# Moving the next tile's transposes, rounding and low part ahead of the roots and the norm, in every z2 block of a gMLP kernel

## The chip, the cores and the metric

The kernel runs on one core of a Trainium2 chip. The core has five engines, each with an instruction queue of its own that runs in order: TensorE (PE) for matrix products, VectorE (DVE), ScalarE (ACT), GpSimd (POOL) and SyncE (SP). In this kernel SP, and POOL for stores, mainly issue DMA transfers between the main memory and the on-chip memory. Engines wait for one another by semaphores. The metric is the device time of one execution in microseconds (us).

## The reference

The network is a layer norm with modulation, a state-space convolution (SSM), a second modulated layer norm, and a gMLP over 2048 tokens of 576 channels. The change lies in the gMLP:

```python
def _B_ref(x, w_in, w_sp, b_sp, w_out):
    z = _gelu(jnp.einsum("bsd,df->bsf", x, w_in))
    z1 = z[..., :Fh]
    z2 = _layernorm(z[..., Fh:], axis=-1)
    g = jnp.einsum("ts,bsf->btf", w_sp, z2) + b_sp[None, :, None]
    return jnp.einsum("bsf,fd->bsd", z1 * g, w_out)
...
h = _layernorm(x, axis=-1) * (1 + cb) + sb
x = x + gb * _B_ref(h, B_w_in, B_w_sp, B_b_sp, B_w_out)
```

Fh is 2304. All is in float32; the kernel reaches that precision with products of 16-bit pairs, a rounded high part and the low part that is left.

## The kernel before

The program has three stages: the SSM (up to about 440 us of the span), **phase A**, which makes the normalised z2 of all tokens and prepares weights (to about 680 us), and **phase B**, which makes z1, the spatial product and the output.

Phase A goes over 16 blocks of 128 tokens, b = 0 to 15. A block has these steps:

- `x1_load` (SP) fetches the 576 channels of a block's rows, four blocks ahead. The rows of blocks 0 to 3 are not loaded that way; they lie together in one large tile, `x1f`, in the pool `xz`. From block 8 on, the same pool's memory takes blocks of the spatial weights (`block_load`).
- `ln2_stats` and `roots` (DVE) make mean and inverse root of the rows' layer norm, and `ln2_rows` (DVE) applies it, two blocks ahead.
- `turn` (PE) transposes the normalised rows of the next block, in five products, into the accumulator tile `pt`, of which there is one. `turn_hi` (ACT) rounds them to 16 bits into the tile `nt`; `turn_lo` (DVE) subtracts to get the low part, and POOL stores `nt` (`n_d` in the profile) for phase B.
- `z2_mm(b, h)` (PE) makes 512 columns of z2 (256 for h = 4) in 14 products from `nt` and the weights `wz`; `z2_gelu(b, h)` (ACT) moves them through the gelu into the z2 tile, 2304 columns wide. z2 tiles come from the pool `zp`, which has two buffers, taken in turn.
- `z2_stats` (DVE) gathers the statistics of the z2 tile in six pieces; `roots(b-1, b+2)` makes the inverse root for the z2 tile of block b-1 and for the rows of block b+2 in one run of 16 small instructions; for even tiles `z2_diff` (DVE) forms a difference of the two halves; `z2_norm` (ACT) normalises the tile in place.
- `z2_store` (POOL) issues two transfers that bring the tile to main memory (`z_d` in the profile). Only when they have landed is its buffer free.

The loop body of block b therefore works on tile b, finishes tile b-1 and prepares the rows of b+1 and b+2. Between these steps stand side jobs, called by `do(b, k)` at six places: scaling and splitting of other weights (`side_sum`, `side_hi`, `side_lo`, `win_scale`, `scales_sp`), squares of weights for their norms (`norm_sp`, `norm_out` on ACT, at A0, ahead of the block's first gelu; their loads are issued at A1 of the block before), and the spatial weights' split (`wsp_sums`, `wsp_hi`, `wsp_lo`). The place `PE` holds the small products with `ones` that add up squares over partitions, and the few DVE instructions behind them.

In phase A the object `self.nc` is `self.tied`: the planner keeps every instruction of an engine in program order. Their line in the profile is L132, that of the helper, so that they are told apart by tile names: `z` is a z2 tile (written by the gelu from `pz`, by the norm from `z`), `nt` the rounded rows, `vh`, `rq`, `rx`, `r`, `nm` are the roots, `n` the normalised rows, `bsz` the z2 statistics, `wsst` the weights that are squared.

Before the change, block 1 has an order of its own: there `turn`, the second gelu, `turn_hi` and `turn_lo` stand ahead of `roots`. In all later blocks they stand behind `z2_norm`.

Of the kernel before, what the change touches and what calls it, by code (L numbers as in the profile page):

```python
# [9 lines left out]
F32 = mybir.dt.float32  # L10
# [12 lines left out]
FH = 2304  # L23
# [779 lines left out]
class Mlp:  # L803
# [419 lines left out]
    def z2_gelu(self, b, h):  # L1223
        n = min(512, FH - 512 * h)
        if h == 0:
            self.zs[b] = self.zp.tile([128, FH], F32, name="z2")
            self.bz[b] = self.ap.tile([128, 6, 6], F32, name="bsz")
        self.nc.scalar.activation(self.zs[b][:, 512 * h:512 * h + n], self.pzs.pop((b, h))[:, :n], AF.Gelu_apprx_tanh,
                                  scale=self.wcol(5 + h, INV_IN))
# [24 lines left out]
    def phase_a(self):  # L1254
        self.prods, self.z1s, self.n2, self.bsp, self.gbs, self.wfs = {}, {}, {}, {}, {}, {}
        ap = self.ap = self.pool(self.c2, "ap", 2)
        cpa = ExitStack()
        self.pa = self.pool(cpa, "pa", 6, space=PSUM)
        self.ps1 = lambda: self.pa.tile([128, 512], F32, name="pz")
        self.zp = self.pool(self.c2, "zp", 2)  # L1260
        self.wp = self.pool(self.ctx, "wp", 7, side="right")

        self.fp = self.pool(self.ctx, "fp", 1, side="right")
        self.wso = ap.tile([128, 4, 10, 128], F16, name="wso", bufs=1)
        self.nc, plain = self.tied, self.nc
        self.nc.vector.memset(self.wso[64:, :, 9], 0.0)

        LD, PE, A0, A1, V0, V1 = range(6)
        sides = [[[] for _ in range(6)] for _ in range(17)]

        def side(b, k, fn, *a):
            sides[b][k].append((fn, a))

        def do(b, k):
            for fn, a in sides[b][k]:
                fn(*a)

        for q in range(5):
            side(2 * q, LD, self.side_load, q)
            side(2 * q + 1, A0, self.side_sum, q)  # L1280
            side(2 * q + 1, PE, self.win_scale, q)
            side(2 * q + 1, A1, self.side_hi, q)
            side(2 * q + 1, V1, self.side_last, q)
            side(2 * q + 1, V1, self.side_lo, q, 0)
            side(2 * q + 2, V0, self.side_lo, q, 1)
        for h in range(2):
            side(1, LD, self.bsp_load, ap, h)
            side(2, A0, self.norm_bsp, h)
        for i in range(8):
            side(2 + i // 2, A1, self.wsp_load, 0, i, ap)  # L1290
            side(3 + i // 2, A0, self.norm_sp, 0, i)
        for i in range(12):
            side(6 + i // 2, A1, self.out_load, ap, i)
            side(7 + i // 2, A0, self.norm_out, i)
        for i in range(6):
            side(12 + i // 2, A1, self.wsp_load, 1, i, ap)
            side(13 + i // 2, A0, self.norm_sp, 1, i)
        side(13, V1, self.sums_out)
        side(14, PE, self.scales_out)
        side(6, V1, self.sums_sp, 0)  # L1300
        side(7, PE, self.scales_sp, 0)
        side(11, PE, self.scales_gate, 0)
        for i in range(7):
            side(9 + i, V0, self.wsp_sums, i)
            side(9 + i, A1, self.wsp_hi, 0, i)
            side(9 + i, V1, self.wsp_lo, 0, i)
            side(8 + i, V1, self.block_load, 0, i)
        side(10, LD, self.z1_rows, 0)
        side(11, LD, self.bias_load, 0)
        for f in (0, 9, 1):  # L1310
            side(12, LD, self.z1_load, 0, f)

        self.turn(0)
        self.turn_hi(0)
        self.x1_load(4)
        self.turn_lo(0)
        self.start_lo(3)
        do(0, LD)
        self.z2_mm(0, 0)
        self.start_sum(4)  # L1320
        self.z2_gelu(0, 0)
        self.z2_mm(0, 1)
        self.win_scale(9)
        self.start_hi(4)
        self.z2_gelu(0, 1)
        self.ln2_rows(1)
        self.z2_mm(0, 2)
        self.start_lo(4)
        self.z2_gelu(0, 2)
        self.z2_mm(0, 3)  # L1330
        self.turn(1)
        self.turn_hi(1)
        self.z2_gelu(0, 3)
        self.turn_lo(1)
        self.z2_mm(0, 4)
        self.ln2_stats(2)
        self.roots(x=2)
        self.ln2_rows(2)
        self.z2_stats(0, 0, 1, 2, 3)
        self.z2_gelu(0, 4)  # L1340
        self.ln2_stats(3)
        self.z2_stats(0, 4)
        for b in range(1, 16):
            do(b, LD)
            self.z2_mm(b, 0)
            do(b, A0)
            self.z2_gelu(b, 0)
            self.z2_stats(b - 1, 5)
            if b == 1:
                do(b, PE)  # L1350
                self.z2_mm(b, 1)
                self.turn(b + 1)
                self.z2_gelu(b, 1)
                self.turn_hi(b + 1)
                self.turn_lo(b + 1)
            self.roots(b - 1, b + 2 if b + 2 < 16 else None)
            if b % 2:
                self.z2_diff(b - 1)
            self.z2_norm(b - 1)
            if b + 2 < 16:  # L1360
                self.ln2_rows(b + 2)
            if b + 4 < 16:
                self.x1_load(b + 4)
            if b > 1:
                do(b, PE)
                self.z2_mm(b, 1)
                if b + 1 < 16:
                    self.turn(b + 1)
                self.z2_gelu(b, 1)
            self.z2_store(b - 1)  # L1370
            do(b, V0)
            self.z2_stats(b, 0, 1)
            if 2 < b + 1 < 16:
                self.turn_hi(b + 1)
                self.turn_lo(b + 1)
            self.z2_mm(b, 2)
            self.z2_gelu(b, 2)
            do(b, A1)
            self.z2_mm(b, 3)
            self.z2_stats(b, 2, 3)  # L1380
            self.z2_gelu(b, 3)
            if b + 3 < 16:
                self.ln2_stats(b + 3)
            do(b, V1)
            self.z2_stats(b, 4)
            self.z2_mm(b, 4)
            self.z2_gelu(b, 4)
        cpa.close()
        self.z2_stats(15, 5)
        self.roots(15)  # L1390
        self.z2_norm(15)
        self.z2_store(15)
        self.nc = plain
        self.c2.close()
# [334 lines left out]
```

## Time and profile before

| | us |
|---|---|
| median of 3 runs | 1783.14 (1782.89 to 1784.71) |
| the profiled execution | 1782.85 |
| its span, first to last instruction | 1781.1 |
| PE busy | 1693.0 |
| DVE busy | 1127.6 |
| ACT busy | 784.4 |
| POOL busy | 223.7 |

A row of the timeline has the start in us from the span's start, the duration, the engine, the line, the operation, what it writes and reads with shapes, and how many instructions were merged. In brackets stands how long the engine had been idle before, and what ended the wait. A row of the view of waits has who waited for whom, the total, how many times, and the longest. A row of the DMA view has a transfer, the queue, how many, the size of one and the median time from issue to landing.

### The profile page before, as it was taken

What the parts mean: (1) busy time and instruction counts of PE and PEld (TensorE: products, weight loads), DVE (VectorE), ACT (ScalarE), POOL (GpSimd) and SP (SyncE); (2) the same over time, 40 slices, a digit from 0 to 9 for tenths busy, and PEclk for the clock granted to TensorE, in tenths of its full rate; (3) what the DMA queues carried; (4) which work ended last, traced back from release to release, by engine and by line L of the source; (5) the groups of instructions that cost most, each with busy time, mean ns of one, the idle gap of its engine ahead of it and who ended that gap; (6) DMA issues with size and microseconds to landing.
All of it is one profiled execution on the core that took longest, in us unless ns stands there. A gap on an engine that the chain in (4) does not pass through costs nothing.

```text
span 1781.1 us, 34047 instructions
## 1 busy us (share of the span) xinstructions
PE 1693.0 (95%) x14202; PEld 1195.6 (67%) x14202; DVE 1127.6 (63%) x2242; ACT 784.4 (44%) x1023; POOL 223.7 (13%) x350
## 2 busy tenths in 40 slices
PE   5688999997999999999999999999999999999999
PEld 1344555565455456877787777887778787787787
DVE  7988999868888997998783544483222274222322
ACT  5668999854576665554341322241211132011110
POOL 1221232342122110000000000000000000000000
PEclk8788999998999999999999999999999999999999
DMA  8457545799588888786554666563655572545520
GB/s 277 139 207 235 145 129 161 192 248 301 163 278 264 277 235 259 284 283 245 207 206 166 238 234 222 202 255 101 216 203 187 176 271 70 182 174 175 201 84 27
DMA packets 145866, 361.57 MB, mean 203 GB/s; under 512 B 23296, under 2 KB 59008, under 8 KB 143792
## 3 DMA queue, kind: packets, MB, share of 16 engines
q1 hardware_dynamic: 103104, 167.30, 29.8%
q0 software_dynamic: 33120, 153.95, 25.8%
q10 hardware_dynamic: 9488, 38.16, 5.4%
q8 instruction: 111, 1.82, 0.4%
q14 instruction: 43, 0.35, 0.1%
HBM read 256.86 MB, written 93.05 MB: 196 GB/s over the span
## 4 chain that ended last, share of the span: by engine, by line
PE 53%; issue 10%; DVE 9%; DMA 7%; ACT 2%; POOL 1%; SPq 0%; POOLq 0%; ACTq 0%; DVEq 0%
PE ps L1451 9%; PE ps L1453 9%; PE ps L1452 9%; PE ps L1416 9%; PE pz L132 4%; PE ps L1505 3%; PE ps L1506 3%; PE ps L1503 3%; DMA zset<-set_d 2%; DVE zset L1134 2%; DMA z_d<-z 1%; DVE bsz L132 1%; DVE gt L1466 1%; ACT z L132 1%; DMA gbs<-in_w_out 1%
## 5 line engine op out<-in xcount | busy, mean ns | idle before, releaser
L1451 PE MATMUL ps<-wsp,zset 128*128 128x256 f16 x2016 | 550.2, 273 | 2.9 <-DVE gt L1466 2.8
L1453 PE MATMUL ps<-wsp,zset 128*128 128x256 f16 x2016 | 550.1, 273 | 1.4 <-DVE zset L1134 1.3
L1452 PE MATMUL ps<-wsp,zset 128*128 128x256 f16 x2016 | 550.1, 273 | 0.0
L132 PE MATMUL pz<-wz,nt 128*128 128x512 f16 (+1 forms) x1120 | 224.2, 360 | 8.1 <-ACT nt L132 6.7
L1466 DVE SCALAR_TENSOR_TENSOR gt<-ps,sc,bsp 128x512 f32<-128x512 f32 x33 | 24.7, 749 | 317.2 <-PE ps L1453 317.2
L1416 PE MATMUL ps<-n2q,wf 128*128 128x512 f16 x1008 | 223.1, 379 | 0.0
L1451 PEld LDWEIGHTS <-zset 128*128 128x128 f16 x2016 | 197.7, 98 | 29.8 <-DVE gt L1466 3.0
L1452 PEld LDWEIGHTS <-zset 128*128 128x128 f16 x2016 | 197.5, 98 | 26.2
L1453 PEld LDWEIGHTS <-zset 128*128 128x128 f16 x2016 | 197.5, 98 | 25.0 <-DVE zset L1134 2.0
L132 PEld LDWEIGHTS <-nt 128*128 128x128 f16 x1120 | 109.5, 99 | 114.1 <-ACT nt L132 8.4
L1416 PEld LDWEIGHTS <-wf 128*128 128x128 f16 x1008 | 98.6, 98 | 111.8
L1428 POOL DMA_DIRECT2D zset<-set_d x96 | 50.8, 529 | 969.3 <-PE ps L1453 742.5
L1421 ACT ACTIVATE z<-ps,sc 128x512 f32<-128x512 f32 x56 | 37.8, 681 | 280.5 <-PE ps L1416 278.0
L1505 PE MATMUL ps<-wout,z 128*128 128x288 f16 x448 | 127.6, 286 | 0.0
L1506 PE MATMUL ps<-wout,z 128*128 128x288 f16 x448 | 127.6, 286 | 0.0
L1503 PE MATMUL ps<-wout,z 128*128 128x288 f16 x448 | 126.0, 286 | 1.0 <-ACT ot L1513 1.0
L1466 DVE SCALAR_TENSOR_TENSOR gt<-ps,sc,gt 128x512 f32<-128x512 f32 (+1 forms) x165 | 111.8, 694 | 5.4
L1134 DVE TENSOR_TENSOR zset<-raw,zset 128x1024 f16<-128x1024 f32 x48 | 58.5, 1220 | 75.2 <-ACT zset L1133 75.2
L1133 ACT ACTIVATE zset<-raw 128x1024 f16<-128x1024 f32 x48 | 50.3, 1050 | 99.6 <-PE ps L1453 69.7
L132 ACT ACTIVATE z<-pz,sc 128x512 f32<-128x512 f32 (+1 forms) x80 | 49.4, 647 | 54.1 <-DMA z_d<-z 43.6
L1521 DVE TENSOR_TENSOR ot<-ot,ps 128x288 f32<-128x288 f32 x31 | 14.0, 452 | 78.7 <-ACT ot L1513 78.7
L369 PE MATMUL ps<-ln_x,r1t 128*128 128x288 f32 x128 | 42.7, 490 | 18.9 <-issue 12.4
(360 smaller groups left out, 2830.6 us busy)
## 6 DMA issues: line engine op xcount, KB each, us to landing
zset<-set_d POOLq DMA_DIRECT2D x96, 896.0 KB, 4.8
set_d<-zset ACTq DMA_DIRECT2D x36, 896.0 KB, 5.8
raw<-z_d SPq DMA_DIRECT2D x48, 512.0 KB, 4.6
wf<-win_d SPq DMA_DIRECT2D x72, 320.0 KB, 3.5
raw<-in_w_spT SPq DMA_DIRECT2D x43, 512.0 KB, 6.3
z_d<-z POOLq DMA_DIRECT2D x32, 576.0 KB, 7.6
u_d<-st1o POOLq DMA_DIRECT2D x16, 576.0 KB, 4.5
u<-u_d SPq DMA_DIRECT2D x36, 256.0 KB, 4.7
```

The source lines that it names most:

```text
L132: return self.tc.keep_in_program_order(f(*a, **k))
L1133: nc.scalar.activation(o[:, k, 0], t, AF.Copy)
L1134: nc.vector.tensor_tensor(o[:, k, 1], t, o[:, k, 0], op=ALU.subtract)
L1416: nc.tensor.matmul(pm.rearrange("p (t c) -> p t c", t=4), w[:, kw], self.n2[q][:, :, kn], start=i == 0, stop=i == len(Z1) - 1)
L1428: self.nc.gpsimd.dma_start(o, self.set_d[n // 4, n % 4])
L1451: T.matmul(pm, z[:, a, 0, c], w[:, b, 0], start=i + half == 0, stop=False, skip_group_check=True)
L1452: T.matmul(pm, z[:, a, 0, c], w[:, b, 1], start=False, stop=False, skip_group_check=True)
L1453: T.matmul(pm, z[:, a, 1, c], w[:, b, 0], start=False, stop=i == 7, skip_group_check=True)
L1466: V.scalar_tensor_tensor(dst, pm, inv, to, op0=ALU.mult, op1=ALU.add)
L1503: T.matmul(pl, p[:, 1, ts], w[:, 0, hs], start=st, stop=sp)
L1505: T.matmul(pa, p[:, 0, ts], w[:, 0, hs], start=st, stop=False)
L1506: T.matmul(pa, p[:, 0, ts], w[:, 1, hs], start=False, stop=sp)
```

## The change

The steps of block 1 become those of every block: the products for the second 512 columns, the transposes of the next block's rows, the second gelu, `turn_hi` and `turn_lo` now stand ahead of `roots`, `z2_diff` and `z2_norm` in all blocks. The side jobs at the place `PE` move with them. `turn_lo` issues the store of `nt` on POOL, which so moves ahead of the z2 store of the same block. The z2 tiles of blocks 2 and 5 are no longer taken from `zp` but laid into `x1f`, whose rows of blocks 0 to 3 are used up by then.

```diff
     def z2_gelu(self, b, h):
         n = min(512, FH - 512 * h)
         if h == 0:
-            self.zs[b] = self.zp.tile([128, FH], F32, name="z2")
+            self.zs[b] = self.x1f.rearrange("p b d -> p (b d)") if b in (2, 5) else self.zp.tile([128, FH], F32, name="z2")
             self.bz[b] = self.ap.tile([128, 6, 6], F32, name="bsz")
...
             do(b, A0)
             self.z2_gelu(b, 0)
             self.z2_stats(b - 1, 5)
-            if b == 1:
-                do(b, PE)
-                self.z2_mm(b, 1)
+            do(b, PE)
+            self.z2_mm(b, 1)
+            if b + 1 < 16:
                 self.turn(b + 1)
-                self.z2_gelu(b, 1)
+            self.z2_gelu(b, 1)
+            if b + 1 < 16:
                 self.turn_hi(b + 1)
                 self.turn_lo(b + 1)
             self.roots(b - 1, b + 2 if b + 2 < 16 else None)
...
             if b + 4 < 16:
                 self.x1_load(b + 4)
-            if b > 1:
-                do(b, PE)
-                self.z2_mm(b, 1)
-                if b + 1 < 16:
-                    self.turn(b + 1)
-                self.z2_gelu(b, 1)
             self.z2_store(b - 1)
             do(b, V0)
             self.z2_stats(b, 0, 1)
-            if 2 < b + 1 < 16:
-                self.turn_hi(b + 1)
-                self.turn_lo(b + 1)
             self.z2_mm(b, 2)
```

## The prediction

> **What bounds the kernel now.** I read the page first, then the waits by engine in the stretch of phase A (436 to 700 us, the z2 loop), then its timeline on each engine.
>
> ```profile
> PE 1693.0 (95%) x14202; PEld 1195.6 (67%) x14202; DVE 1127.6 (63%) x2242; ACT 784.4 (44%) x1023; POOL 223.7 (13%) x350
> ```
>
> TensorE (PE) is busy for 95% of the span, so time is gained or lost only where it stands still. In phase A it waits for this:
>
> ```profile
> PE pz L132 <- ACT nt L132: 6.7, 5, 4.2
> PE pz L132 <- DVE nt L132: 1.3, 1, 1.3
> ```
>
> The columns are the total, the times and the longest. The z2 products `pz` wait 8.0 us in all for `nt`, the rounded transposed rows that `turn_hi` writes on ScalarE (ACT) and `turn_lo` on VectorE (DVE); 4.2 of it in one place. The PE timeline shows that place, and an undisturbed block:
>
> ```profile
> 488.18 4.88 PE L132 MATMUL pz<-wz,nt 128*128 128x512 f16 x14 [4.21 <-ACT nt L132]
> ...
> 629.01 0.71 PE L132 MATMUL pt<-ident,n 128*128 128x128 f32 x5
> 629.55 13.78 PE L132 MATMUL pz<-wz,nt 128*128 128x512 f16 x70
> 643.17 0.71 PE L132 MATMUL pt<-ident,n 128*128 128x128 f32 x5
> ```
>
> An undisturbed block takes 14.16 us (643.17 less 629.01). Of its 70 matmuls 56 are wide and 14 half as wide, so 14 wide ones take 13.78 x 14/63 = 3.06 us; those after the 4.21 us wait took 4.88, so that wait cost 1.8 us more. The whole prize of the change is then 8.0 + 1.8 = 9.8 us.
>
> PE is not the only engine near its limit there. In the stretches from 437 to 680 us DVE is busy 214.6 of 243 us, and ACT waits longest for something that the change touches:
>
> ```profile
> sum 243.00, PE 233.38 PEld 121.91 DVE 214.60 ACT 153.24 POOL 52.38; mean PE 14.59 PEld 7.62 DVE 13.41 ACT 9.58 POOL 3.27
> ```
>
> ```profile
> ACT z L132 <- DMA z_d<-z: 43.6, 12, 7.2
> ```
>
> Twelve of the blocks' first gelus wait for the store of an older z2 tile, because the pool `zp` has two buffers: block b's gelu needs the buffer of block b-2. So there is a ring now: gelu(b,0), norm(b-1), store(b-1), landing, gelu(b+1,0). It just fits into 14.16 us, because norm stands right behind the first gelu on ACT.
>
> **The change part by part.** All of phase A runs in program order on each engine, and the timelines have the code's order. The change puts gelu(b,1), turn_hi(b+1) (ACT) and turn_lo(b+1) (DVE) ahead of roots(b-1) (DVE) and norm(b-1) (ACT). No instruction is added or removed. Block 1 has the new order already, and shows what it does:
>
> ```profile
> 466.42 1.02 DVE L132 TENSOR_TENSOR nt<-pt,nt 128x512 f16<-128x512 f32 x2
> ...
> 472.40 1.35 ACT L132 ACTIVATE z<-z,nm,r 128x1152 f32<-128x1152 f32 x1 [9.32 <-DVE z L132]
> ...
> 475.18 2.03 POOL L132 DMA_DIRECT2D z_d<-z  x2 [6.67 <-ACT z L132]
> ...
> 483.53 0.69 ACT L132 ACTIVATE z<-pz,sc 128x512 f32<-128x512 f32 x1 [2.61 <-DMA z_d<-z]
> ```
>
> turn_lo(2) at 466.42, norm(0) 6.0 us later after 9.32 us in which ACT stood still, the store at 475.18, gelu(2,0) at 483.53. From turn_lo to the next block's gelu: 17.1 us, longer than a block.
>
> *The store ring.* Its terms, with G the start of gelu(b,0):
>
> ```profile
> 453.89 0.77 ACT L132 ACTIVATE nt<-pt 128x512 f16<-128x512 f32 x2 [2.88 <-PE pt L132]
> ...
> 454.69 1.02 DVE L132 TENSOR_TENSOR nt<-pt,nt 128x512 f16<-128x512 f32 x2 [1.96 <-ACT nt L132]
> ...
> 635.56 0.67 ACT L132 ACTIVATE z<-pz,sc 128x512 f32<-128x512 f32 x1
> 636.13 0.75 ACT L132 ACTIVATE nt<-pt 128x512 f16<-128x512 f32 x2
> ```
>
> A gelu takes 0.57 us until the next ACT instruction, so turn_hi starts at G + 1.14. turn_lo starts 0.80 later (454.69 less 453.89) and takes 1.02, 1.05 with the step to the next instruction: the roots start at G + 2.99. DVE is in order, so nothing overtakes the waiting turn_lo: behind it stand the roots, the difference, the rows of block b+2 and the statistics.
>
> ```profile
> 629.97 0.32 DVE L132 BATCH_NORM_AGGREGATE mvx<-bsz 128x2 f32<-128x36 f32 x1
> ...
> 633.34 2.31 ACT L132 ACTIVATE z<-z,nm,r 128x2304 f32<-128x2304 f32 x1 [2.93 <-DVE nm L132]
> ...
> 635.94 2.00 POOL L132 DMA_DIRECT2D z_d<-z  x2 [9.86 <-ACT z L132]
> ```
>
> An odd tile: roots to norm 3.37, norm to store 2.60.
>
> ```profile
> 643.52 0.32 DVE L132 BATCH_NORM_AGGREGATE mvx<-bsz 128x2 f32<-128x36 f32 x1
> ...
> 647.99 0.81 DVE L132 SCALAR_TENSOR_TENSOR n<-x1t,mvx,mrow 128x576 f32<-128x576 f32 x1
> 648.17 1.35 ACT L132 ACTIVATE z<-z,nm,r 128x1152 f32<-128x1152 f32 x1 [2.23 <-DVE z L132]
> ...
> 650.96 2.01 POOL L132 DMA_DIRECT2D z_d<-z  x2 [11.32 <-ACT z L132]
> ...
> 660.75 0.69 ACT L132 ACTIVATE z<-pz,sc 128x512 f32<-128x512 f32 x1 [3.59 <-DMA z_d<-z]
> ```
>
> An even tile (with z2_diff): 4.65, 2.79, and from the store to the freed buffer 9.79. For this last term the trace has these ends:
>
> ```profile
> 589.90 2.02 POOL L132 DMA_DIRECT2D z_d<-z  x2 [11.08 <-ACT z L132]
> ...
> 597.91 0.69 ACT L132 ACTIVATE z<-pz,sc 128x512 f32<-128x512 f32 x1 [1.46 <-DMA z_d<-z]
> ...
> 605.48 2.02 POOL L132 DMA_DIRECT2D z_d<-z  x2 [8.10 <-ACT z L132]
> ...
> 617.34 0.69 ACT L132 ACTIVATE z<-pz,sc 128x512 f32<-128x512 f32 x1 [4.26 <-DMA z_d<-z]
> ```
>
> 8.0 and 11.9 us (block 1's store took 8.35). I take 9.8, which lies midway and is a row of the blocks in question. Then G(b+1) - G(b) is 2.99 + 3.37 + 2.60 + 9.8 = 18.8 us where tile b-1 is odd, and 2.99 + 4.65 + 2.79 + 9.8 = 20.2 where it is even. PE can't go faster: the next products need turn_hi, which follows G.
>
> Where does the ring bind? The tiles of blocks 2 and 5 now lie in `x1f`. The two `zp` buffers go to 0, 1, 3, 4, 6, 7, 8, 9 and so on in turn, so up to block 7 a tile waits for the store of block b-3, long landed. From block 8 it waits for that of b-2 again. So eight steps, G(7) to G(15), four of each kind: 4 x 18.8 + 4 x 20.2 = 156.0 us.
>
> *Blocks 2 to 7: the loads.* Here a second ring remains. x1_load(b+4) waits on SyncE's queue until the rows of b+2 are read, which is behind the roots; behind it stand two loads whose squares (`norm_sp`, `norm_out`) ACT runs before gelu(b+1,0).
>
> ```profile
> 618.37 0.33 SPq L132 DMA_DIRECT2D x1t<-x_d  x1
> 618.74 0.90 SPq L132 DMA_DIRECT2D wsst<-in_w_out  x2
> ```
>
> ```profile
> wsst<-in_w_spT SPq DMA_DIRECT2D x14, 512.0 KB, 6.5
> ...
> wsst<-in_w_out SPq DMA_DIRECT2D x12, 432.0 KB, 5.0
> ```
>
> ```profile
> 480.73 0.19 ACT L132 ACTIVATION_READ_ACCUMULATOR wsst<-wsst 128x1 f32 x1
> ...
> 555.16 0.69 ACT L132 ACTIVATE z<-pz,sc 128x512 f32<-128x512 f32 x1 [2.10 <-DMA z_d<-z]
> ...
> 674.50 0.69 ACT L132 ACTIVATE z<-pz,sc 128x512 f32<-128x512 f32 x1 [4.37 <-DMA z_d<-z]
> ```
>
> From the roots' start the rows begin after 4.47 us (647.99 less 643.52), 3.2 without the difference (4.65 less 3.37 is its 1.28); 0.8 for the first instruction, 0.4 from one issue to the next, 6.5 or 5.0 to land, then two squares of 1.04 (0.9 for `w_out`, estimated by its 27/32 of the size). A step is 2.99 + 3.2 + 0.8 + 0.4 + 6.5 + 2.1 = 16.0 us from an even block, 17.3 from an odd one, and 14.2 from block 6, whose loads are of `w_out`. No store holds G(2): it follows the squares that end at 480.9. G(7) = 480.9 + 16.0 + 17.3 + 16.0 + 17.3 + 14.2 = 561.7, where it was 555.16. So the 4.2 us stall is not won but spread: the old wait goes, and late squares and products behind them take its place.
>
> *The sum.* G(15) = 561.7 + 156.0 = 717.7, against 674.50: 43.2 us later. Behind G(15) the same work is left on ACT and DVE (gelus, the last norm and store, the sets of phase B), so it shifts as a whole. PE has a little room there:
>
> ```profile
> 697.83 0.27 PE L1451 MATMUL ps<-wsp,zset 128*128 128x256 f16 x1
> 697.94 0.27 PE L1452 MATMUL ps<-wsp,zset 128*128 128x256 f16 x1
> ```
>
> ```profile
> 708.95 0.95 DVE L1134 TENSOR_TENSOR zset<-sum,zset 128x768 f16<-128x768 f32 x1
> ```
>
> The spatial products start at 697.83 and use a set for 42 matmuls, 0.11 us apart: the fourth is needed at 697.83 + 3 x 42 x 0.11 = 711.7 and is built, from the last store, at 709.9. That is 1.8 us of cover; after it phase B is bound by PE as now. Result: 43.2 - 1.8 = 41 us.
>
> What I cost at nothing: writing z2 tiles into `x1f` (the rows of block 3 are read in block 1, before 480.9); the store of `nt`, now ahead of the z2 store on GpSimd's queue (0.6 us, issued at about G + 3, while the z2 store comes at G + 9 or later); the scales that move ahead of the roots on DVE (1.6 us in blocks 3, 5, 7, 9, below the time that DVE then stands idle; if that cover is gone, 1 to 2 us each).
>
> The Trainium skill prices a store otherwise: "DMA: Bandwidth & Descriptors", section "Anatomy of one DMA — SWDGE (gpsimd) path", puts a transfer issued by GpSimd at about 2.0 us plus its bytes at 436 KB per us. For the two halves of a tile on the same engines that is an estimate of 4.7 us, where this trace shows no pair under 8.0; by it the store ring would take 13.7 and 15.1 us and no longer decide.
>
> **The rivals.** A) *The gain.* Each store is back before it is needed, PE's waits on `nt` vanish, and the 9.8 us are won: 1782.85 - 9.8 = 1773. For it speaks that the change aims right at the waiting rows and that block 2's store wait goes. It decides only if the store ring fits a block: a landing under 14.16 - (8.96 + 10.43)/2 = 4.5 us, and DVE, busy nine tenths, must not wait for ACT. No row has that. B) *Loss and gain cancel*: the ring costs no more than about 10 us, within 0.2% of 1783. It would need landings about 5 us, and loads faster than their medians. C) *Stores land fast because the blocks are longer*, 5.5 us or less, and the load ring sets all steps: G(7) to G(15) is then 15.5 + 14.2 + 15.5 + 14.2 + 15.5 (`w_out`) + 16.0 + 17.3 + 16.0 = 124 us, the end 32 us earlier than forecast: about 1792. The Trainium skill's formula named above would give this case; this trace shows no landing so short.
>
> **How the numbers follow.** The profiled execution took 1782.85 us (span 1781.1), and the median of the runs shown is 1783.14; they agree to 0.02%, so I add to 1782.85: 1782.85 + 41 = 1824. Chances: forecast 0.85, A 0.06, B 0.03, C 0.06. The forecast's ends: eight landings of 8.0 instead of 9.8 give 14 us less, four loads landing in 5.0 instead of 6.5 another 6; eight of 11.9 give 17 more. That is 1804 to 1841. The range holds the forecast's whole chance, which leaves 0.15 out. Faster by over 0.2% (about what a measurement of this kernel can tell): 0.06; within: 0.03; slower: 0.91.
>
> **What would show it.** Right: from block 8 to 15, gelu(b,0) starts about 18.8 and 20.2 us apart, each ended by the store of b-2; DVE waits for `nt` in most blocks; norm waits for DVE; PE waits several us for `nt` in each block from 8; blocks 3 to 7 show no store wait on ACT but waits for `wsst`. The second half of the span is as before. Wrong: blocks 14.2 us apart from block 8 on, or stores landing in 5 us, or PE waits on `nt` gone.

## The result and the profile after

| | before | after |
|---|---|---|
| median, us | 1783.02 (1782.53 to 1784.71) | 1834.86 (1831.22 to 1836.06) |
| ratio | 1 | 1.0281 (95%: 1.0259 to 1.0302) |
| profiled execution, us | 1782.85 | 1836.06 |
| its span, us | 1781.1 | 1834.3 |

The change costs 52 us; 41 were forecast. The page of after, busy times:

```profile
PE 1708.8 (93%) x14202; PEld 1198.2 (65%) x14202; DVE 1126.3 (61%) x2242; ACT 785.4 (43%) x1023; POOL 223.3 (12%) x350
```

DVE, ACT and POOL do the same work in the same time. PE is busy 15.8 us longer with the same instructions, and stands still for the rest. The waits of after in phase A (436 to 760 us), first PE's, then ACT's and DVE's; the columns are the total, the times and the longest:

```profile
PE pz L132 <- ACT wso L132: 20.9, 4, 6.6
PE pz L132 <- ACT nt L132: 15.5, 6, 5.5
PE pz L132 <- DVE sums L132: 7.8, 1, 7.8
...
ACT z L132 <- DMA z_d<-z: 39.2, 8, 5.9
ACT z L132 <- DVE z L132: 38.2, 6, 9.3
ACT z L132 <- DVE nm L132: 32.4, 7, 5.4
...
DVE nt L132 <- ACT nt L132: 58.2, 15, 7.5
```

PE waited 8.0 us for `nt` before; now 15.5, and 28.7 more ahead of the small sums (`wso` and `sums`). The norm (ACT `z`) waits 70.6 us for DVE, and 10.3 more in the two tiles in `x1f` (`xz`); DVE itself waits 58.2 us for `nt`. In phase A of before (436 to 700 us) the norm waited 27.8 us for DVE, and there were hardly any waits of DVE for `nt` or of PE ahead of the small sums:

```profile
DVE nt L132 <- ACT nt L132: 2.6, 2, 2.0
...
PE pz L132 <- ACT wso L132: 0.8, 1, 0.8
```

The timeline of after in block 8, whose tile b-1 is odd, shows the whole ring:

```profile
587.37 1.26 ACT L132 ACTIVATE z<-pz,sc 128x512 f32<-128x512 f32 x2 [5.87 <-DMA z_d<-z]
588.53 0.76 ACT L132 ACTIVATE nt<-pt 128x512 f16<-128x512 f32 x2
589.32 1.02 DVE L132 TENSOR_TENSOR nt<-pt,nt 128x512 f16<-128x512 f32 x2 [7.50 <-ACT nt L132]
590.37 0.32 DVE L132 BATCH_NORM_AGGREGATE mvx<-bsz 128x2 f32<-128x36 f32 x1
593.83 2.31 ACT L132 ACTIVATE z<-z,nm,r 128x2304 f32<-128x2304 f32 x1 [4.54 <-DVE nm L132]
596.43 2.02 POOL L132 DMA_DIRECT2D z_d<-z  x2 [5.02 <-ACT z L132]
...
607.49 1.26 ACT L132 ACTIVATE z<-pz,sc 128x512 f32<-128x512 f32 x2 [4.89 <-DMA z_d<-z]
```

Both gelus start when the store of tile 6 is back (587.37); turn_hi follows 1.16 us later, turn_lo at 589.32 after DVE stood still for 7.50, roots at 590.37 (G + 3.00), norm 3.46, store 2.60 later, and gelu(9,0) starts 11.06 us after that store. The rows of the next block, with an even tile, end the same way:

```profile
618.01 2.02 POOL L132 DMA_DIRECT2D z_d<-z  x2 [6.47 <-ACT z L132]
...
627.83 1.26 ACT L132 ACTIVATE z<-pz,sc 128x512 f32<-128x512 f32 x2 [3.89 <-DMA z_d<-z]
...
726.68 1.26 ACT L132 ACTIVATE z<-pz,sc 128x512 f32<-128x512 f32 x2 [5.24 <-DMA z_d<-z]
```

A store at G + 10.52, the next G 9.82 after it. The last row is gelu(15,0): 52.2 us later than before's 674.50. In this run the first stage had ended 2.0 us earlier (the rounding of the first tile starts at 438.27, before at 440.26), so that from there to gelu(15,0) the loss is 54.2. It is complete where phase A ends. In phase B nearly the same work follows; the waits there, of after and then of before (line numbers moved by 8):

```profile
PE ps L1443 <- DVE gt L1458: 4.0, 2, 3.7
PE ps L1445 <- DVE zset L1134: 3.4, 5, 1.3
```

```profile
PE ps L1451 <- DVE gt L1466: 2.8, 1, 2.8
PE ps L1453 <- DVE zset L1134: 1.3, 1, 1.3
```

The first spatial product starts at 746.96, 49.1 us later than before's 697.83, so 3.1 us less late than gelu(15,0); these waits take 3.3 us back.

In the odd blocks 3 and 5 the store ring is not the limit; there the second gelu waits for PE. Timeline of after, block 5, PE with the two gelus (`xz` is the tile in `x1f`):

```profile
526.79 0.59 PE L132 MATMUL pz<-acc,ones 128*128 128x1 f32 x2 [4.56 <-ACT wso L132]
527.24 6.12 PE L132 MATMUL pz<-wz,nt 128*128 128x512 f16 x14
528.71 0.68 ACT L132 ACTIVATE xz<-pz,sc 128x512 f32<-128x512 f32 x1
533.39 0.69 ACT L132 ACTIVATE xz<-pz,sc 128x512 f32<-128x512 f32 x1 [4.01 <-PE pz L132]
```

On PE the small sums stand ahead of the products of the second gelu, and stood there before the change too. In block 5 of before PE passes them without a wait:

```profile
521.53 0.38 PE L132 MATMUL pz<-acc,ones 128*128 128x1 f32 x2
521.77 3.18 PE L132 MATMUL pz<-wz,nt 128*128 128x512 f16 x14
```

What is new is that ACT comes later to the squares that they add up. They wait 4.56 us for ACT (`wso` is what `side_sum` writes while it squares a weight), and the 14 products behind them take 6.12 us instead of 3.06: gelu(5,1), and with it turn_hi, turn_lo and the roots, comes 4.68 us after gelu(5,0), not 0.57. The windows of after over these products and over the rest of the block give the granted clock (the third number from the end):

```profile
527.20:533.40 6.20, 6.20 (x17) 2.42 (x18) 1.64 (x10) 2.19 (x6) 0.00 (x0) 0.52 0.93 241
533.40:547.00 13.60, 13.60 (x74) 7.07 (x73) 10.95 (x33) 7.80 (x13) 2.56 (x3) 1.00 0.43 129
```

The array ran at 0.52 of its clock behind the wait and at full clock afterwards. Over the whole run the z2 products took 236.1 us, 224.2 before; that is 11.9 of the 15.8 us by which PE is busy longer. The Trainium skill, "TensorE: Matmul & The Clock Gate", section "Part 1: The HAM clock gate (the "warmup" mystery)", says that the clock is halved after an idle window of about 3.4 us and comes back after a busy one of that length, and that the windows run free. The 4.56 us wait and the 0.52 agree with it; the slow stretch was 6.1 us here, longer than one such window.

### The profile page after: what moved, and what is told of

It is laid out like the page before. It is cut to its first block, busy times and chain, and to the rows that moved or that the text cites. A ratio compares the mean times of both kernels' runs of the same rounds, so it can differ in the third digit from the quotient of the medians.

```text
span 1834.3 us, 34042 instructions
## 1 busy us (share of the span) xinstructions
PE 1708.8 (93%) x14202; PEld 1198.2 (65%) x14202; DVE 1126.3 (61%) x2242; ACT 785.4 (43%) x1023; POOL 223.3 (12%) x350
## 4 chain that ended last, share of the span: by engine, by line
PE 45%; DVE 6%; issue 5%; DMA 4%; ACT 1%; SPq 0%; POOL 0%; DVEq 0%; ACTq 0%; POOLq 0%
PE ps L1443 9%; PE ps L1445 9%; PE ps L1444 9%; PE ps L1408 9%; PE ps L1498 3%; PE ps L1495 3%; PE ps L1497 3%; DVE zset L1134 2%; DMA z_d<-z 1%; DVE gt L1458 1%; DMA gbs<-in_w_out 1%; DMA raw<-z_d 1%; DMA zset<-set_d 1%; ACT zset L1133 1%; DMA gbs<-mod_d 0%
## 5 line engine op out<-in xcount | busy, mean ns | idle before, releaser
L132 PE MATMUL pz<-wz,nt 128*128 128x512 f16 (+1 forms) x1120 | 236.1, 372 | 15.5 <-ACT nt L132 15.5
L132 PEld LDWEIGHTS <-nt 128*128 128x128 f16 x1120 | 112.8, 102 | 130.1 <-ACT nt L132 17.1
L1413 ACT ACTIVATE z<-ps,sc 128x512 f32<-128x512 f32 x56 | 37.8, 680 | 279.9 <-PE ps L1408 271.3
L132 ACT ACTIVATE z<-pz,sc 128x512 f32<-128x512 f32 (+1 forms) x70 | 41.7, 634 | 47.1 <-DMA z_d<-z 39.2
```

Of the source, the lines that this page charges most:

```text
L132: return self.tc.keep_in_program_order(f(*a, **k))
```

## The experiments

My theory: turn_lo ahead of the roots makes DVE, which runs in order, wait for the new block's `nt`, and so puts norm and store of the old tile into a ring with the freed buffer. The rivals: the loads and their squares set the steps; PE's waits at the small sums do; the store's landing is slowed by traffic; the tiles in `x1f` cost something. The table has, beside the times, how long each profiled run takes from turn_hi of tile 2 to that of tile 8, and on to tile 15, so that the length of the first stage is left out. The ratio is to before on the same chip.

| kernel | median us | ratio (95%) | 2 to 8 | 8 to 15 | 2 to 15 |
|---|---|---|---|---|---|
| before | 1783.02 | 1 | 96.9 | 104.9 | 201.8 |
| after | 1834.86 | 1.0281 (1.0259 to 1.0302) | 106.0 | 142.4 | 248.4 |
| e1_old_from_7 | 1792.25 | 1.0045 (1.0025 to 1.0065) | 107.9 | 105.5 | 213.4 |
| e2_third_buffer | 1828.78 | 1.0256 (1.0236 to 1.0277) | 107.6 | 120.4 | 228.0 |
| e3_low_behind_rows | 1790.05 | 1.0043 (1.0027 to 1.0059) | 93.3 | 111.7 | 205.0 |
| e4_buffers_only | 1781.30 | 0.9984 (0.9967 to 1.0000) | 94.2 | 104.9 | 199.1 |
| e5_third_buffer_early | 1818.71 | 1.0202 (1.0152 to 1.0252) | 107.5 | 119.8 | 227.3 |
| e6_sums_late | 1809.04 | 1.0148 (1.0115 to 1.0181) | 98.9 | 116.8 | 215.7 |
| e7_third_store | 1870.22 | 1.0491 (1.0447 to 1.0535) | 108.4 | 164.5 | 272.9 |
| e8_store_from_act | 1852.43 | 1.0391 (1.0357 to 1.0426) | 116.4 | 139.5 | 255.8 |
| e9_low_behind_three | 1785.42 | 1.0017 (1.0005 to 1.0029) | 88.7 | 103.5 | 192.3 |
| e10_block2_only | 1779.74 | 0.9983 (0.9970 to 0.9995) | 96.6 | 102.9 | 199.5 |

Between tiles 2 and 15 lie 46.6 us of the loss, 9.1 up to tile 8 and 37.5 behind it. The last step, from turn_hi of tile 15 to gelu(15,0), adds 7.6 (17.96 us against 10.40).

### e1: the old order from block 7 on

The new order only in blocks 1 to 6; blocks 7 to 15 keep the order of before, with the tiles in `x1f` as changed.

```diff
-            if b == 1:
+            if b < 7:
                 do(b, PE)
...
-            if b > 1:
+            if b > 6:
                 do(b, PE)
...
-            if 2 < b + 1 < 16:
+            if 7 < b + 1 < 16:
                 self.turn_hi(b + 1)
```

> The changed kernel, but with the order of before in blocks 7 to 15 (the buffers as changed). Theory (a ring through the store: gelu, turn_hi, turn_lo, roots, norm, store, landing, next gelu, binding only where a tile waits for the store of two blocks before): the first gelus of blocks 8 to 15 go back to about 14.4 to 15 us apart from 20.4, so about 40 of the 52 us go and 8 to 14 stay from blocks 2 to 6: 1791 to 1797. Rival (the new order costs about the same in every block, by DVE waiting for ACT, whatever the buffers): 5 of 13 blocks keep it, so about 20 of 52 us stay: 1803.

1792.25 us. The steps from tile 8 on are those of before (105.5), those up to tile 8 as long as in after (107.9). So about 43 of the 52 us come from blocks 7 to 15, where two buffers go in turn, and some 9 from blocks 2 to 6. PE's waits in e1, phase A:

```profile
PE pz L132 <- ACT wso L132: 14.2, 3, 6.5
PE pz L132 <- ACT nt L132: 1.6, 3, 0.7
```

What is left is the wait of the small sums, not the wait for `nt`.

### e2 and e5: a third buffer

After, but three z2 tiles lie in the memory in which weights are staged, so that most tiles of blocks 8 to 15 need not wait for the store of b-2. In e2 these are tiles 9, 12 and 15:

```diff
-            self.zs[b] = ... if b in (2, 5) else self.zp.tile([128, FH], F32, name="z2")
+            self.zs[b] = ... if b in (2, 5) else self.stg.tile([128, 5, 512], F32, name="wst")... if b in (9, 12, 15) else self.zp.tile([128, FH], F32, name="z2")
```

> The changed kernel with a third buffer for blocks 9 to 15 too: the z2 tiles of blocks 9, 12 and 15 lie in the staging tile of the weights, which is free by then; nothing else is changed. Store ring: no gelu from block 9 on waits for a store, the steps fall from 20.4 to what the ring through the loads allows, 14.2 to 17.3 us, G(8) to G(15) from 139 to about 110 us, the time to about 1800 to 1808. Rival (DVE waiting for ACT's rounding is the cost itself, stores or not): DVE waits as long as now, and the time stays within 10 us of 1835.

The steps fell from 142.4 to 120.4 as expected, the time by 6 us only, far from the forecast. By the time alone the rival would hold (within 10 us of 1835), but DVE's wait for `nt` fell from 58.2 to 37.8 us. Two rows of e2's waits, PE's longest single one and one of SyncE's queue, and then that queue's timeline:

```profile
PE ps L1408 <- DMA wf<-win_d: 17.1, 1, 17.1
...
SPq L132 <- DMA z_d<-wst: 25.6, 2, 23.3
```

```profile
699.66 27.47 SPq L132 DMA_DIRECT2D raw<-z_d  x3
```

The first loads of phase B (`raw`) come behind the store of a tile from the staging memory (`z_d<-wst`), whose memory is loaded anew; the queue stands 23.3 us at it, and the weights of the z1 products (`wf`) stand behind on the same queue. So e2 took one wait away and made another of 17.1 us at the border to phase B; it could not give the price of the ring. e5 uses tiles 9, 10 and 13 instead, whose stores are back before phase B:

```diff
-... if b in (9, 12, 15) else ...
+... if b in (9, 10, 13) else ...
```

> As the third buffer before, but the tiles in the weights' staging are 9, 10 and 13 in place of 9, 12 and 15, so that the last tile's store no longer holds the memory that phase B's first loads take. With 9, 12 and 15 the gelus G(8) to G(15) took 112 us, as the ring through the loads has it, yet 17 us were lost behind phase A, where PE waited for a weight load queued on SP behind a load that waited for the store of tile 15. Store ring: G(8) to G(15) stays near 112 us and the 17 us go: 1808 to 1815. Rival (the 17 us are owed to something else at the start of phase B, for example the late norm of tile 15): the wait stays, 1825 or more.

The 17.1 us are gone, the steps stay at 119.8, and 1818.71 is 4 us above the upper end of what was expected, which is less than the 5.6 us between its two runs. In the whole timeline of e5 only one gelu of blocks 8 to 15 is still ended by a store, that of block 8:

```profile
592.29 1.27 ACT L132 ACTIVATE z<-pz,sc 128x512 f32<-128x512 f32 x2 [5.93 <-DMA z_d<-z]
```

Comparing with after, the store in the ring costs 22.6 us from tile 8 on (142.4 less 119.8). The blocks still take about 17 us without it (119.8 / 7), so something else holds them. PE's waits of e5 name it:

```profile
PE pz L132 <- ACT wso L132: 21.3, 4, 6.6
PE pz L132 <- DVE sums L132: 7.7, 1, 7.7
```

### e6: the small sums behind the third product group

e5, with the place `PE` moved behind the third products in all blocks but the first.

```diff
-            do(b, PE)
+            if b == 1:
+                do(b, PE)
             self.z2_mm(b, 1)
...
             self.z2_mm(b, 2)
+            if b > 1:
+                do(b, PE)
             self.z2_gelu(b, 2)
```

> The kernel with the third buffer in tiles 9, 10 and 13, and the small sums (the place PE with its products with ones) moved behind the block's third product. In the changed kernel PE stands 28.7 us in front of those sums in five blocks, since the squares they add up come late on ACT, and the second product, the transposes and so the second gelu stand behind them. Theory (these waits are the second price, as the second gelu and turn_hi wait for PE there, by 2.6 to 4 us in blocks 3 and 5): the waits of PE on the squares go, the steps of odd blocks get shorter by 2 to 4 us, 8 to 20 us less than with the third buffer alone: 1790 to 1803. Rival (PE only waits there because it is early; the ring through the loads sets the steps): within 4 us of the third buffer alone.

The direction was right, the size at the low end: 9.7 us below e5 (11.6 from tile 2 to 15), where 8 to 20 were expected. The time is 6 us above the expected range, which was set before e5 was measured. PE's waits of e6:

```profile
PE pz L132 <- DVE sc L132: 7.0, 4, 4.4
...
PE pz L132 <- ACT wso L132: 1.6, 2, 0.8
```

The 21.3 us for `wso` are 1.6 now, and 7.0 came in their place: the sums' accumulator is emptied late by DVE (`sc`), and PE needs it. So PE's waiting at the sums is a part of the loss. In neither kernel do they stand behind the third products: e6 takes out a wait that the change brought by making ACT later, not a move of the sums on PE.

### e3 and e9: the low part behind the rows

e3 leaves all of the change but one line: from block 2 on, turn_lo stands behind the roots and the rows on DVE. Two buffers, the sums where the change has them.

```diff
             if b + 1 < 16:
                 self.turn_hi(b + 1)
+            if b == 1:
                 self.turn_lo(b + 1)
             self.roots(b - 1, b + 2 if b + 2 < 16 else None)
...
                 self.ln2_rows(b + 2)
+            if 2 < b + 1 < 16:
+                self.turn_lo(b + 1)
```

> The changed kernel, but turn_lo stands behind roots, difference and ln2_rows on DVE from block 2 on; on ACT the second gelu and turn_hi stay ahead of the norm. Theory (the price is DVE's in-order wait for turn_hi, which puts the roots and so norm and store into the ring): the roots no longer follow G, the ring is 1.78 + 2.6 to 2.8 + about 10 = 14.4 to 15 us, and most of the loss goes: 1783 to 1797. Rival (what costs is ACT's order, the norm behind the second gelu and turn_hi, or the small sums ahead of the second product on PE): the loss stays above 30 us, over 1813.

1790.05 us: 45 of the 52 us are gone by moving this one step, and of the 46.6 us of phase A all but 3.2. DVE's wait, in the stretch of 436 to 700 us of e3:

```profile
DVE nt L132 <- ACT nt L132: 9.0, 6, 2.5
```

58.2 us have become 9.0. The waits for the small sums shrink with it, from 28.7 to 7.2 us, so they are for the most part a consequence: what they wait for is itself behind the late norm and roots. e9 puts all three together, the low part behind the rows (in block 2 right behind the roots), the third buffer of e5 and the late sums of e6:

```diff
             self.roots(b - 1, b + 2 if b + 2 < 16 else None)
+            if b == 2:
+                self.turn_lo(b + 1)
...
                 self.ln2_rows(b + 2)
+            if 2 < b < 15:
+                self.turn_lo(b + 1)
```

> All three prices taken out at once: the second gelu and turn_hi stay ahead of the norm on ACT, but turn_lo stands behind the rows on DVE (in block 2 behind the roots), a third buffer in blocks 9 to 15 as before (tiles 9, 10, 13), the small sums behind the third product. Theory (the loss is DVE's wait for turn_hi in the ring, the store ring, and PE's waits on the sums; what is left is DVE's own work): from the rounding of block 2 to that of block 15 there were 201.8 us before, now 194 to 199, and the time is 3 to 8 us below the kernel before. Rival (moving turn_hi ahead of the norm costs by itself, through the later norm): 203 to 207 us there, as with the low part behind the rows and two buffers (205.0), and 2 to 6 us above the kernel before.

Phase A is now 9.5 us shorter than before (192.3 against 201.8), better than the 194 to 199 expected. Yet the time is 0.17% above before, where 3 to 8 us below were expected: the phase came as the theory has it, the time as the rival has it. The timeline of e9 at the start of phase B, ACT and PE:

```profile
694.01 0.69 ACT L1421 ACTIVATE z<-ps,sc 128x512 f32<-128x512 f32 x1 [7.11 <-DMA z_d<-z]
...
696.43 0.39 PE L1451 MATMUL ps<-wsp,zset 128*128 128x256 f16 x1 [3.86 <-ACT zset L1133]
```

The z1 products started at 672.46, 7.2 us earlier than before (679.70), but the spatial products only at 696.43, 1.4 us earlier (697.83): a z1 tile waited 7.11 us for memory from which a z2 tile was still being stored. So 5.8 of the 7.2 us are lost at the border, with a late store ahead of them, and the run ends 2.6 us later than before's; where the 4.0 us behind the first spatial product go was not followed. The same wait for memory stands in e5 (7.5 us) and e6 (7.1), and neither in before nor in after.

### e4: the tiles in x1f alone

Before, with only the tiles of blocks 2 and 5 moved.

> The kernel before with the z2 tiles of blocks 2 and 5 in the first rows' tile, the order of before kept. The first gelu of block 2 no longer waits for a store, but its second gelu and turn_hi still stand behind norm(1), which waits for the roots on DVE until the same time; the stall of PE ahead of block 3 stays within 1 us of 4.2. Time 1780 to 1784, the same as before. Rival (the wait for the store is what holds PE there): the stall goes, 5 to 6 us faster, 1777.

1781.30 us, ratio 0.9984 (0.9967 to 1.0000): as expected no loss, at most a small gain. The PE timeline shows that the 4.2 us stall ahead of block 3's products stays:

```profile
485.85 5.55 PE L132 MATMUL pz<-wz,nt 128*128 128x512 f16 x14 [4.23 <-ACT nt L132]
```

### e7 and e8: the landing of the store

e7 is after with the first half of each z2 tile stored a second time, to a scratch tensor that nothing reads:

```diff
+        self.nc.gpsimd.dma_start(self.z2_e[:, b // 4, :, 2 * (b % 2), b % 4 // 2].rearrange("f p c -> p f c"), z[:, 0])
```

> The changed kernel with one more store of each z2 tile: its first half goes once more, to a scratch tensor that nothing reads, issued on GpSimd behind the two stores. The tile's buffer is free only when all three have landed, 1.0 us of issue and some 1 to 2 us of transfer later. Store ring: the steps G(7) to G(15) grow by those 2 to 3 us each, eight times, and the steps of blocks 2 to 7 do not: 1850 to 1860. Rival (stores are hidden, DVE's wait sets the steps): within 5 us of 1835.

The steps from tile 8 to 15 grew by 22.1 us, 3.2 for each of seven, those up to tile 8 by 2.4. So the time from store to freed buffer is in the ring from block 8 on, and hardly before. A rival in which the loads set the steps would not give such a split. The total grew by 35, more than expected, partly by a wait of 8.1 us at the start of phase B (z1 tiles waiting for the same memory). e7's timeline in blocks 8 and 9:

```profile
603.42 2.02 POOL L132 DMA_DIRECT2D z_d<-z  x2 [5.01 <-ACT z L132]
605.44 1.01 POOL L132 DMA_DIRECT2D z_e<-z  x1
616.81 1.27 ACT L132 ACTIVATE z<-pz,sc 128x512 f32<-128x512 f32 x2 [7.62 <-DMA z_e<-z]
```

13.4 us from the first issue to the gelu, for three transfers. e8 issues the stores from ScalarE instead of GpSimd:

```diff
-            self.nc.gpsimd.dma_start(self.z2_d[...], z[:, h])
+            self.nc.scalar.dma_start(self.z2_d[...], z[:, h])
```

> The changed kernel with both halves of each z2 store issued from ScalarE's own queue, right behind the norm, in place of GpSimd's. An issue there takes 0.35 us in place of 1.0. Store ring: whatever the time from norm to freed buffer loses, each of the eight steps G(7) to G(15) loses; if the landing itself is no slower that is 1 to 2.5 us each, 1815 to 1827. Rival (the landing is set by the data alone): within 4 us of 1835.

A miss: 1852.43 us, slower than after by 18, where I had expected a gain. Two rows of e8's timeline on ACT's sequencer, each a pair of issues:

```profile
516.42 3.12 ACTq L132 DMA_DIRECT2D z_d<-xz  x2
...
592.02 1.79 ACTq L132 DMA_DIRECT2D z_d<-z  x2
```

Issuing a pair takes ACT 1.0 to 3.1 us, and gelu and norm stand behind it. The steps up to tile 8, where no store is in the ring, grew by 10.4 us. Those from tile 8 to 15 fell by 2.9, as the ring has it, but by less than expected. At the start of phase B PE waited 8.7 us for weights (`wf`), 0.7 in after. The landing wasn't shorter in the first blocks of the ring (11.8 us for the pair at 592.02, 13.4 for the next); it was in the last three (7.1 to 8.4, in after 9.1 to 10.2). The core moved 292 and 255 GB/s during the first two landings and 163 to 167 during the last three, so the shorter landings go with less traffic; that the traffic is their cause is not shown.

### e10: the new order in block 2 alone

Before, with the tiles in `x1f`, the new order in block 2 only, turn_lo there right behind the roots, and block 3's small sums behind its third product group. This takes the one large stall (4.21 us) without a ring.

```diff
-            if b == 1:
+            if b < 3:
                 do(b, PE)
...
                 self.turn_hi(b + 1)
+            if b == 1:
                 self.turn_lo(b + 1)
             self.roots(b - 1, b + 2 if b + 2 < 16 else None)
+            if b == 2:
+                self.turn_lo(b + 1)
```

> The kernel before with the z2 tiles of blocks 2 and 5 in the first rows' tile and one block reordered: in block 2 alone the second product, the transposes, the second gelu and turn_hi stand ahead of the norm, turn_lo right behind the roots, and in block 3 the small sums behind the third product. Theory (the 4.2 us stall of PE in front of block 3 comes from turn_hi behind a norm that waits for DVE; nothing on DVE gets later here): the stall and the slow products behind it go, 6 us; PE is then that much ahead of DVE and waits more for nt in blocks 9 to 14, which gives back 2 to 5: 1 to 4 us below the kernel before. Rival (DVE sets the pace of phase A, so all is given back): within 1 us.

1779.74 us, ratio 0.9983 (0.9970 to 0.9995): 2.1 us below before on the same chip, as expected, and the lowest median here; the difference is no larger than what the prediction took as the bound of what a measurement can tell. The PE timeline of e10:

```profile
475.59 13.78 PE L132 MATMUL pz<-wz,nt 128*128 128x512 f16 x70
489.20 0.71 PE L132 MATMUL pt<-ident,n 128*128 128x128 f32 x5
...
501.03 6.22 PE L132 MATMUL pz<-wz,nt 128*128 128x512 f16 x28 [3.41 <-ACT nt L132]
```

The stall ahead of block 3 is gone, the 70 products across that place run through; 3.41 us of it come back a block later. e4 alone reads the same (0.9984, and 199.1 us against 199.5 from tile 2 to 15), so what the reordering of block 2 adds to the buffers was not told apart.

## Why the prediction was right, and what it mis-sized

**What bounds the kernel; the prize.** Right in the main: PE's standstill sets most of the time, but PE was also slower behind its waits (236.1 us for the z2 products, not 224.2), which the prediction counted in the prize and not in the loss. The waits for `nt` that the change aimed at did not go but doubled (8.0 to 15.5 us).

**The store ring.** Right in mechanism. Its main signs are there: gelu(b,0) about 20 us apart from block 8, each ended by a store, DVE waiting for `nt` in nearly every block, the norm waiting for DVE, no store wait of the first gelus in blocks 3 to 7. One sign came only in part: from block 8 on PE waits for `nt` in five blocks, 0.9 to 5.5 us, not several us in each. e3 (turn_lo out of the ring), e5 (the buffer out) and e7 (the landing longer) each moved the steps in the way it says. The part from G to the store came as worked out: odd tiles 8.90 to 9.06 against 8.96, even ones 10.43 to 10.52 against 10.43, but for block 7 (11.98). The term that was too small is *from the store to the freed buffer*: 9.8 was taken, and after's eight were 11.74, 11.06, 9.82, 11.02, 10.50, 9.13, 10.21 and 10.21, a mean of 10.46, so 5.3 us over the eight steps. In before the six that the gelus of blocks 9 to 15 show have a mean of 9.97, so the change hardly slowed the landing itself. The ends taken for it, 8.0 and 11.9, are those of blocks 9 to 15; earlier in the trace of before two stores took 12.8 us (from 500.76) and 14.2 (from 529.15) until the gelu. G(7) to G(15) took 163.0 us instead of 156.0; block 7 accounts for 1.5 of the other 1.7, since its second gelu came 2.04 us after the first, behind the small sums, not 0.57.

**Blocks 2 to 7.** Here the mechanism was wrong and the sum near by chance. The gelus start at 478.84 for block 2 and 563.65 for block 7, so 84.8 us instead of 80.8; but the single steps were 14.87, 20.46, 14.54, 20.67 and 14.27 where 16.0, 17.3, 16.0, 17.3 and 14.2 stood. Errors of opposite signs partly cancel. The loads, which were to set the steps, were hardly late. After's waits of the squares for them, in all of phase A, are these:

```profile
ACT wsst L132 <- DMA wsst<-in_w_out: 2.7, 3, 1.8
...
ACT wsst L132 <- DMA wsst<-in_w_spT: 2.0, 3, 1.5
```

In the five steps they are 0.17, 1.51, 0, 0.30 and 0 us. What sets the steps from the even blocks is the start of the ring, from the gelu to the norm, and ACT's own work in order behind it. In block 4, with its first gelu at 514.17, the norm starts 6.43 us later:

```profile
520.60 2.31 ACT L132 ACTIVATE z<-z,nm,r 128x2304 f32<-128x2304 f32 x1 [4.54 <-DVE nm L132]
```

From there ACT works without a pause until gelu(5,0) at 528.71. The steps from the odd blocks 3 and 5 were longer because PE waited at the small sums and went on at half clock. The prediction had the place `PE` in its list of *what I cost at nothing*, with 1.6 us on DVE and 1 to 2 us each "if that cover is gone"; what it did not ask is which other engine waits there. That is PE, in front of the very products that the second gelu needs, for squares that ACT now makes later. Up to tile 8, e6 takes 8.6 us off by moving the sums alone; there the steps from blocks 3 and 5 are 17.15 and 17.06.

**Phase B.** 1.8 us of cover were to be given back. PE did start its spatial products 3.1 us earlier against gelu(15,0), and lost 3.3 to the waits for `gt` and the sets.

**The sum.** Forecast 41, measured in the profiled runs 53.2. The difference of 12.2 is 7.0 (store ring) + 4.0 (blocks 2 to 7) - 2.1 (G(2) at 478.84, not 480.9; 2.0 of it is the first stage's earlier end in this run, and not the change) + 1.8 (cover) + 1.0 (the end 53.2 later, gelu(15,0) 52.2), and 0.4 of rounding (43.2 - 1.8 was set down as 41). The time, 1834.86, lies in the range, above its middle because all three doubtful terms fell the same way. The range was made from the landings alone, so that the error in blocks 2 to 7 also fits into it is luck.

**The rivals.** A, the gain, needed landings under 4.5 us; none was under 9.1 in the eight steps of after. C needed 5.5 or less. The formula of the Trainium skill, "DMA: Bandwidth & Descriptors", section "Anatomy of one DMA — SWDGE (gpsimd) path", from which 4.7 us was estimated for a tile, does not hold for this pair beside other traffic: the trace shows 10.46.

How the 46.6 us of phase A divide is shown only in one order of taking them away: the third buffer 21.1 (e5), then the late sums 11.6 (e6), then turn_lo behind the rows 23.4 (e9), which ends 9.5 below before. Taken first and alone, moving turn_lo is worth 43.4 (e3). The parts aren't added up as separate costs, since each hides behind the others.

## What to carry to other kernels

Before a step that waits for new data is moved ahead of a step that frees old data on an in-order engine, write down the ring that this closes (wait, free, transfer, buffer, next data) and add it up; if it is longer than a block and the buffers are two, the pool's depth can set the time, as from block 8 on here, however much room each engine has. Ask of each side job beside the moved steps which engine waits at it, not only which engine does its work. A buffer borrowed to break a ring must be free again where the next phase loads into it.

## What the runs showed of the hardware

- The store of a z2 tile, two transfers of 576 KB issued by GpSimd, took 9.1 to 11.7 us in after's ring from its first issue until the buffer was used again; a third transfer of the same size added 3.2 us to a step.
- The same pair issued from ScalarE held that engine for 1.0 to 3.1 us.
- The clock granted behind a standstill of 4.56 us was 0.52 over 6.2 us, and 14 products took exactly twice 3.06. So that standstill cost 3.1 us beyond its own length.
- The first stage, which is the same code in all kernels here, ended at different times in the profiled runs: the rounding of the first tile started between 437.2 us (e2) and 445.1 (e3). The ends of single profiled runs can differ by as much for that reason alone, so the table compares stretches inside phase A.
